# One-token attention over a 1 GB cache on one core: 64 KB rows, overlapping places, loops over heads

## The chip, the cores and the metric

The kernel runs on one core of a Trainium2 chip. The metric is the device time of one execution in microseconds. The kernel before has a median of 2582.4 us over three runs (2581.64 to 2582.49).

## The reference

One token attends to a cache of 65536 keys and values in each of 32 heads, a small gated MLP runs beside it, and a scalar gate mixes the two. Everything is bfloat16.

```python
B, Sq, D = 1, 1, 512
H, Sk, Dh = 32, 65536, 128          # k_cache, v_cache: [1, 32, 65536, 128], 537 MB each
F = 1792
q = (x @ wq) in 32 heads
p = softmax(q k^T * Dh ** -0.5)     # over 65536 keys, per head
a = (p v, heads side by side) @ wo
b = (silu(x @ w_gate) * (x @ w_up)) @ w_down
g = sigmoid((x * gate_w).sum(-1))
out = g * a + (1 - g) * b           # x = A_x everywhere; B_x is not used
```

K and V are 1073.7 MB, the five weights 13.9 MB. Each byte is read once, and each key and value is used for one query only.

## The kernel before

**Places and loads.** A ring of 20 slots of 8 KB per partition (160 KB) lies in SBUF. `plan_stream` (L25) writes the order of loads out by hand: wq first, then K in pieces of four slots (128 partitions with one contiguous row of 32 KB each, 4 MB), with w_gate, w_up and w_down behind the first K piece. V pieces of the same form follow two heads late, one after each K piece; wo comes just ahead of the last head's V, and the last V piece is cut into smaller ones. wo is read in rows of 1 KB (L184). SyncE walks this list (L206 to L228): before each load it waits until the ring's slots are free, which for K is when DVE has turned the piece (`ktdone`) and for V when PE has used it (`pvdone`).

**K.** Per unit of 64 keys a partition, DVE turns 32x32 blocks of 4-byte words, that is pairs of bf16 (L336, 4096 words a partition), into one of two `kt` buffers. PE then takes the turned K as the stationary operand, 128x128 at a time, and streams four columns of q past it (L412). `qd` holds q spread over columns so that the four partition groups of a turned block stay apart. A head's scores are 128x512 in PSUM, in one of two banks.

**Softmax.** Per head: DVE maximum over the scores (L310), GpSimd all-reduce over partitions (L245), ScalarE exponential with the row sum (L261), all-reduce of the sums (L247). DVE then shuffles the probabilities with 16 small copies (L320) into the layout in which V's rows stand.

**V.** V rows are the stationary operand, 128x128, and one column of probabilities streams past (L429); all 512 row groups of a head add up in one PSUM column. DVE scales the column by the inverse sum (L327).

**Projection, MLP, output.** The MLP runs early: up and gate after K unit 3, down after unit 4 (L375 to L390). The scaled head outputs are the stationary column in 32 matmuls of 512 columns against wo (L394), 31 of them between the last V pieces. One DVE instruction on one partition mixes both parts (L350) and ScalarE's queue stores 1x512 as one row (L264).

All engines run straight code: every head's instructions are written out. PE has 33062 matmuls and as many weight loads.

Of the kernel before, what the change touches and what calls it, by code (L numbers as in the profile page):

```python
# [5 lines left out]
P = 128  # L6
PC = 64
NR = PC // 4
UNIT = PC * 128
HU = UNIT // 2  # L10
RING = 20
ROW = 2
NSEM = 16

ALU = mybir.AluOpType
ACT = mybir.ActivationFunctionType
BF16 = mybir.dt.bfloat16
# [5 lines left out]


def plan_stream(H, NP):  # L25

    w = 2 * ROW  # L30
    per = 2 * NP // w
    ks = [("k", h, u * w, w) for h in range(H) for u in range(per)]
    vs = [("v", h, u * w, w) for h in range(H) for u in range(per)]
    vs = vs[:-1] + [("v", H - 1, 2 * NP - 4, 2), ("v", H - 1, 2 * NP - 2, 1), ("v", H - 1, 2 * NP - 1, 1)]
    lag = 2 * per
    items = [("wq", 0, 0, 4)]
    n = 0
    for i, it in enumerate(ks):
        items.append(it)
        if i == 0:  # L40
            items += [("wg", 0, 0, 2), ("wu", 0, 0, 2), ("wd", 0, 0, 2), ("pad", 0, 0, 2)]
        if i >= lag:
            items.append(vs[n])
            n += 1
    while n < len(vs):
        if vs[n][1:3] == (H - 1, 0):
            items.append(("wo", 0, 0, 4))
        items.append(vs[n])
        n += 1
    return items  # L50


def bass_gated_mix__mha_block_cached__swiglu_ffn__decode_kernel(
# [16 lines left out]
    Dc = D // P  # L70
    FC = F // P
    NP = S // P // PC
    SCALE = float(Dh) ** -0.5
    assert Dh == 128 and D == 512 and F % P == 0 and NP * PC == 512

    items = plan_stream(H, NP)

    dmas = []
    place = {}
    landed = {}  # L80
    owner = [None] * RING
    pos = 0
    for kind, h, u0, nu in items:
        done = 0
        while done < nu:
            k = min(nu - done, RING - pos % RING)
            slots = [(pos + j) % RING for j in range(k)]
            if kind != "pad":
                waits = [owner[s] for s in slots if owner[s] is not None]
                n = len(dmas)  # L90
                dmas.append((kind, h, u0 + done, k, slots[0], waits))
                for j in range(k):
                    place[(kind, h, u0 + done + j)] = slots[j]
                    landed[(kind, h, u0 + done + j)] = n
                    owner[slots[j]] = (kind, h, u0 + done + j)
            pos += k
            done += k
    kseq = {("k", h, u): h * NP + u // 2 for h in range(H) for u in range(2 * NP)}
    vseq = {("v", h, u): h * NP + u // 2 for h in range(H) for u in range(2 * NP)}

    with ExitStack() as ctx:
# [6 lines left out]
        def sem(name):  # L108
            return ctx.enter_context(nc.semaphore(name))

        psS = psum("psS", [P, 2, 512], F32)
        psO = psum("psO", [P, 2, 512], F32)
# [3 lines left out]
        psB = psum("psB", [P, 512], F32)  # L116

        ring = sb("ring", [P, RING * HU], BF16)
        kt = sb("kt", [P, 2, UNIT // 2], U32)
        sel = sb("sel", [P, 4, 128], BF16)  # L120
        ones1 = sb("ones1", [P, 2], BF16)
        xrow = sb("xrow", [P, D], BF16)
        gwrow = sb("gwrow", [P, D], BF16)
        xg = sb("xg", [P, D], F32)
        brow = sb("brow", [P, D], F32)
        fin = sb("fin", [P, D], BF16)
# [3 lines left out]
        qd = sb("qd", [P, H, 4, 4], BF16)  # L130
        hbuf = sb("hbuf", [P, 3, 16], F32)
        guT = sb("guT", [P, 16], BF16)
        mxs = sb("mxs", [P, H], F32)
        amx = sb("amx", [P, H], F32)
        nbias = sb("nbias", [P, H], F32)
        rsum = sb("rsum", [P, H], F32)
        Lt = sb("Lt", [P, H], F32)
        Li = sb("Li", [P, H], F32)
        oTn = sb("oTn", [P, H], BF16)
        pa = sb("pa", [P, 2, 512], BF16)  # L140
        pb = sb("pb", [P, 2, 512], BF16)

        s_x = sem("s_x")
        ds = [sem(f"ds{i}") for i in range(NSEM)]
        s_ones = sem("s_ones")
        s_sel0 = sem("s_sel0")
        s_sel = sem("s_sel")
        s_z = sem("s_z")
        s_e1 = sem("s_e1")
        s_xT = sem("s_xT")  # L150
        s_xTb = sem("s_xTb")
        s_q = sem("s_q")
        s_qTb = sem("s_qTb")
        s_qs = sem("s_qs")
        s_qd = sem("s_qd")
        s_h = sem("s_h")
        s_sig = sem("s_sig")
        s_gu = sem("s_gu")
        s_b = sem("s_b")
        s_dch = sem("s_dch")  # L160
        ktdone = sem("ktdone")
        qkdone = sem("qkdone")
        pvdone = sem("pvdone")
        s_mx = sem("s_mx")
        s_ar = sem("s_ar")
        s_nb = sem("s_nb")
        expdone = sem("expdone")
        s_pb = sem("s_pb")
        s_L = sem("s_L")
        s_otn = sem("s_otn")  # L170
        s_y = sem("s_y")
        s_fin = sem("s_fin")
        s_out = sem("s_out")

        xr_dram = A_x.rearrange("a b d -> (a b) d")
        out_dram = out.rearrange("a b d -> (a b) d")
        gw_dram = gate_w.rearrange("(a d) -> a d", a=1)
        w_dram = {
            "wq": A_wq.rearrange("(p c) n -> p (c n)", c=Dc),
            "wg": B_w_gate.rearrange("(p c) f -> p (c f)", c=Dc),  # L180
            "wu": B_w_up.rearrange("(p c) f -> p (c f)", c=Dc),
            "wd": B_w_down.rearrange("(p c) n -> p (c n)", c=FC),
        }
        wo_dram = A_wo.rearrange("(h d) n -> d h n", d=Dh)  # L184

        def at(key, n):
            s = place[key]
            return ring[:, s * HU:s * HU + n]

        wq_ap = at(("wq", 0, 0), Dc * H * Dh).rearrange("p (c n) -> p c n", c=Dc)  # L190
        wg_ap = at(("wg", 0, 0), Dc * F).rearrange("p (c m j) -> p c m j", c=Dc, j=FC)
        wu_ap = at(("wu", 0, 0), Dc * F).rearrange("p (c m j) -> p c m j", c=Dc, j=FC)
        wd_ap = at(("wd", 0, 0), FC * D).rearrange("p (c n) -> p c n", c=FC)
        wo_ap = at(("wo", 0, 0), H * D).rearrange("p (h n) -> p h n", h=H)
        ktb = [kt[:, b, :].bitcast(BF16).rearrange("p (j r m e) -> p j r m e", j=2, r=NR, e=2) for b in range(2)]

        def arrived(eng, key):
            n = landed[key]
            eng.wait_ge(ds[n % NSEM], 16 * (n // NSEM + 1))

        block = ctx.enter_context(nc.Block())

        @block.sync
        def _(sp):
            w = 2 * ROW
            for n, (kind, h, u0, k, s0, waits) in enumerate(dmas):  # L206
                need = {}
                for key in waits:
                    if key in kseq:
                        need["k"] = max(need.get("k", 0), kseq[key] + 1)  # L210
                    elif key in vseq:
                        need["v"] = max(need.get("v", 0), vseq[key] + 1)
                    else:
                        need[key[0]] = 1
                for key, s in (("wq", s_q), ("wg", s_h), ("wu", s_h), ("wd", s_b), ("k", ktdone), ("v", pvdone)):
                    if key in need:
                        sp.wait_ge(s, need[key])
                dst = ring[:, s0 * HU:(s0 + k) * HU]
                if kind in "kv":
                    cache = A_k_cache if kind == "k" else A_v_cache  # L220
                    src = cache[0, h].rearrange("(b p r) d -> b p (r d)", p=P, r=ROW * PC)[
                        u0 // w, :, (u0 % w) * HU:(u0 % w + k) * HU]
                elif kind == "wo":
                    dst, src = wo_ap, wo_dram
                else:
                    src = w_dram[kind]
                    dst = ring[:, s0 * HU:s0 * HU + src.shape[1]]
                sp.dma_start(dst, src).then_inc(ds[n % NSEM], 16)  # L228
                if n == 0:
                    sp.dma_start(xrow[0:1, :], xr_dram).then_inc(s_x, 16)  # L230
                    sp.dma_start(gwrow[0:1, :], gw_dram).then_inc(s_x, 16)

        @block.gpsimd
        def _(pool):
            nc.gpsimd.memset(sel[:], 0.0).then_inc(s_sel0, 1)
            pool.wait_ge(s_sel0, 1)
# [5 lines left out]
            last.then_inc(s_sel, 1)  # L242
            for h in range(H):
                pool.wait_ge(s_mx, h + 1)
                nc.gpsimd.partition_all_reduce(amx[:, h:h + 1], mxs[:, h:h + 1], P, RMAX).then_inc(s_ar, 1)  # L245
                pool.wait_ge(expdone, h + 1)
                nc.gpsimd.partition_all_reduce(Lt[:, h:h + 1], rsum[:, h:h + 1], P, RADD).then_inc(s_L, 1)  # L247
# [218 lines left out]
```

## Time and profile before

| | |
|---|---|
| runs, median | 2582.4 us |
| profiled execution, span from the first to the last instruction | 2580.2 us |
| DMA read from HBM | 1087.64 MB, 422 GB/s over the span |
| busy: PE, DVE, ACT, POOL | 952.7, 1308.7, 33.1, 25.9 us |
| mean granted TensorE clock | 0.516 |
| code fetched (queue 8) | 258 packets, 4.23 MB |
| K loads; V loads of 4 MB | 128; 127 |

The page cuts the span into 40 slices and gives busy tenths, the clock's tenths, the DMA engines' busy share and the rate in each. "DMA share" is a mean over 16 DMA engines. A load is landed when all of them have done their part. SPq rows are SyncE's issuing of loads, with the waits ahead of it. In a group's row "mean ns" is that of one instruction from its start to its modelled end; where instructions overlap, the spacing between their starts is shorter.

### The profile page before, as it was taken

The numbers are of one execution on the slowest core, as the hardware profiler recorded it, in microseconds if no ns is written. First come the engines' busy times: TensorE is split into PE (matmuls) and PEld (weight loads), VectorE is DVE, ScalarE is ACT, GpSimd is POOL, SyncE is SP. The second block draws the span as 40 slices with busy tenths as digits, with TensorE's granted clock in tenths as the row PEclk, the third lists the DMA queues.
The fourth block names the chain that finished last, engine by engine and source line by source line (L and its number), as shares of the span: only waits on it lengthen the run. The fifth ranks groups of instructions, "written<-read, shape, count | busy, mean of one in ns | idle before, by whom it ended". The sixth has DMA issues, their size and how long they took to land.

```text
span 2580.2 us, 67894 instructions
## 1 busy us (share of the span) xinstructions
PE 952.7 (37%) x33062; PEld 915.5 (35%) x33062; DVE 1308.7 (51%) x883; ACT 33.1 (1%) x99; POOL 25.9 (1%) x73
## 2 busy tenths in 40 slices
PE   2443333333333333333334333433343333333334
PEld 2343333333333333333334333333343333333333
DVE  3955554455454545544554445445445554455430
ACT  0000000000000000000000000000000000000000
POOL 0000000000000000000000000000000000000000
PEclk9555555555555555555555555555555555555555
DMA  9999999999999999999999999999999999999997
GB/s 412 423 431 428 429 429 430 429 430 431 428 428 428 430 429 430 430 429 429 428 429 427 427 426 426 425 424 426 429 425 424 425 424 425 427 423 425 424 392 314
DMA packets 42117, 1091.99 MB, mean 423 GB/s; under 512 B 4211, under 2 KB 8310, under 8 KB 8310
## 3 DMA queue, kind: packets, MB, share of 16 engines
q1 hardware_dynamic: 41844, 1087.65, 98.7%
q8 instruction: 258, 4.23, 0.7%
q14 instruction: 13, 0.11, 0.0%
q10 hardware_dynamic: 2, 0.00, 0.0%
HBM read 1087.64 MB, written 0.00 MB: 422 GB/s over the span
## 4 chain that ended last, share of the span: by engine, by line
DMA 74%; issue 9%; PE 8%; DVE 8%; SPq 0%; DVEq 0%
DMA ring<-in_A_k_cache_dram 61%; DMA ring<-in_A_v_cache_dram 14%; DVE kt L336 7%; PE psO L429 5%; PE psS L412 2%; PE psY L394 0%; PE psM L380 0%; PE psB L388 0%; DVE mxs L310 0%; DVE pb L320 0%; SPq L228 0%; DVE Li L325 0%; DVE brow L306 0%; DVE fin L350 0%; DVE oTn L327 0%
## 5 line engine op out<-in xcount | busy, mean ns | idle before, releaser
L336 DVE STREAM_TRANSPOSE kt<-ring 128x4096 uint32<-128x4096 uint32 x256 | 1128.4, 4430 | 1147.8 <-DMA ring<-in_A_k_cache_dram 1147.7
L412 PE MATMUL psS<-qd,kt 128*128 128x4 bf16 x16384 | 478.0, 166 | 1408.1 <-DVE kt L336 1408.1
L412 PEld LDWEIGHTS psS<-qd,kt 128*128 128x128 bf16 x16384 | 456.8, 104 | 1429.5 <-DVE kt L336 1429.5
L429 PE MATMUL psO<-pb,ring 128*128 128x1 bf16 x16384 | 463.8, 165 | 201.7 <-issue 143.1
L429 PEld LDWEIGHTS psO<-pb,ring 128*128 128x128 bf16 x16384 | 451.8, 104 | 207.6 <-issue 164.6
L320 DVE COPY pb<-pa 32x128 bf16<-32x128 bf16 x512 | 154.3, 301 | 10.2 <-PE psO L429 3.7
L327 DVE TENSOR_SCALAR oTn<-psO,Li 128x1 bf16<-128x1 f32 x32 | 7.1, 221 | 83.0 <-PE psO L429 81.9
L257 ACT ACTIVATE nbias<-amx 128x1 f32<-128x1 f32 x32 | 6.5, 203 | 2390.3 <-POOL amx L245 2390.3
L245 POOL PARTITION_ALL_REDUCE amx<-mxs x32 | 11.3, 353 | 2412.6 <-DVE mxs L310 2412.6
L261 ACT ACTIVATE pa<-psS,nbias 128x512 bf16<-128x512 f32 x32 | 22.0, 688 | 1.0
L310 DVE TENSOR_REDUCE mxs<-psS 128x1 f32<-128x512 f32 x32 | 20.9, 653 | 2.0 <-PE psS L412 2.0
L247 POOL PARTITION_ALL_REDUCE Lt<-rsum x32 | 12.3, 386 | 36.4 <-ACT pa L261 36.4
L394 PE MATMUL psY<-ring,oTn 128*1 128x512 bf16 x32 | 10.3, 492 | 0.4 <-DVE oTn L327 0.4
L281 DVE CUSTOM_DVE_ANT_0 xg<-xrow,gwrow 1x512 f32<-1x512 bf16 x1 | 0.9, 874 | 12.7 <-DMA gwrow<-in_gate_w_dram 12.7
L380 PE MATMUL psM<-xTb,ring 128*128 128x1 bf16 x112 | 6.9, 198 | 0.0
L380 PEld LDWEIGHTS psM<-xTb,ring 128*128 128x128 bf16 x112 | 6.8, 159 | 0.0
L261 ACT ACTIVATION_READ_ACCUMULATOR pa<-psS,nbias 128x1 f32 x32 | 6.2, 193 | 0.0
L394 PEld LDWEIGHTS psY<-ring,oTn 128*1 128x1 bf16 x32 | 3.1, 101 | 6.6 <-issue 4.2
L359 PE MATMUL psM<-ones,xrow 1*128 1x1 bf16 x4 | 0.3, 171 | 14.0 <-DMA gwrow<-in_gate_w_dram 14.0
L359 PEld LDWEIGHTS psM<-ones,xrow 1*128 1x128 bf16 x4 | 0.2, 113 | 14.0 <-DMA gwrow<-in_gate_w_dram 14.0
L388 PE MATMUL psB<-ring,guT 128*1 128x512 bf16 x14 | 4.8, 515 | 0.0
L325 DVE RECIPROCAL Li<-Lt 128x1 f32<-128x1 f32 x32 | 4.0, 124 | 0.0
(29 smaller groups left out, 18.2 us busy)
## 6 DMA issues: line engine op xcount, KB each, us to landing
ring<-in_A_k_cache_dram SPq DMA_DIRECT2D x128, 4096.0 KB, 43.5
ring<-in_A_v_cache_dram SPq DMA_DIRECT2D x127, 4096.0 KB, 41.0
ring<-in_A_wq_dram SPq DMA_DIRECT2D x1, 4096.0 KB, 12.8
ring<-in_A_wo_dram SPq DMA_DIRECT2D x1, 4096.0 KB, 46.1
ring<-in_A_v_cache_dram SPq DMA_DIRECT2D x1, 2048.0 KB, 38.5
ring<-in_A_v_cache_dram SPq DMA_DIRECT2D x2, 1024.0 KB, 43.1
ring<-in_B_w_gate_dram SPq DMA_DIRECT2D x1, 1792.0 KB, 26.1
ring<-in_B_w_up_dram SPq DMA_DIRECT2D x1, 1792.0 KB, 29.8
```

What stands on the lines that cost most here:

```text
L245: nc.gpsimd.partition_all_reduce(amx[:, h:h + 1], mxs[:, h:h + 1], P, RMAX).then_inc(s_ar, 1)
L247: nc.gpsimd.partition_all_reduce(Lt[:, h:h + 1], rsum[:, h:h + 1], P, RADD).then_inc(s_L, 1)
L257: nc.scalar.mul(nbias[:, h:h + 1], amx[:, h:h + 1], -SCALE).then_inc(s_nb, 1)
L261: nc.scalar.activation(pa[:, h % 2, :], psS[:, h % 2, :], ACT.Exp, bias=nbias[:, h:h + 1], scale=SCALE, accum_out=rsum[:, h:h + 1]).then_i ...
L310: nc.vector.reduce_max(mxs[:, h:h + 1], psS[:, h % 2, :], AX_X).then_inc(s_mx, 1)
L320: last = nc.vector.tensor_copy(dst, sr)
L327: nc.vector.tensor_scalar(oTn[:, h:h + 1], psO[:, h % 2, h:h + 1], Li[:, h:h + 1], None, ALU.mult).then_inc(s_otn, 1)
L336: nc.vector.transpose(o, src).then_inc(ktdone, 1)
L380: last = nc.tensor.matmul(psM[:, o + j:o + j + 1], w[:, c, :, j], xTb[:, c:c + 1], start=(c == 0), stop=(c == Dc - 1))
L394: last = nc.tensor.matmul(psY[0:1, :], oTn[:, h:h + 1], wo_ap[:, h, :], start=(h == 0), stop=(h == H - 1))
L412: last = nc.tensor.matmul(psS[:, h % 2, col:col + 4], ktb[i % 2][:, je // 2, r, :, je % 2], qd[:, h, je, :], start=(je == 0), stop=(je == 3))
L429: last = nc.tensor.matmul(psO[:, h % 2, h:h + 1], vt[:, r * Dh:(r + 1) * Dh], pb[:, h % 2, col:col + 1], start=(col == 0), stop=(col == 511))
```

## The change

- **Rows and places.** K and V are read as two halves a head, each 128 partitions with one contiguous row of 64 KB (8 MB). There are two K places, at bytes 0 to 64 K and 32 to 96 K of a partition, and two V places, at 96 to 160 K and 112 to 176 K. The places of a pair overlap, so a half may be loaded once the other half's part in the shared bytes has been used. DVE takes each first half's upper part first (`A_ORDER`), and PE's values are cut at 64 and 192 rows, with a semaphore increment at each cut, so that the shared bytes come free first. The first head's K comes as two pieces of 32 KB rows and one of 64 KB.
- **Order of loads.** wq, head 0's K, then K, V, K, V with V one head late; then wo, one row group of wo for the last head, w_gate, the last head's first V half, and w_up, the last V pieces and w_down.
- **Loops.** On PE and DVE heads 1 to 31 are a loop of 31 rounds. The other engines stay written out.
- **K streams.** Now K's turned words are the moving operand, 512 wide, and q is the stationary one: a window of `zq` that puts the four scores of a chunk into its own four rows of PSUM. A chunk is 16 keys a partition, with one DVE transpose of 1024 words and four matmuls; there are four `kt` buffers. A head has 128 score matmuls where it had 512. Scores, probabilities and `psO` have one buffer each.
- **Shuffle.** One DVE transpose of 128x512 replaces the 16 copies.
- **wo in 32 KB rows.** Head outputs are kept as four partial blocks in `lt`, turned on PE by an identity at the end, and projected with 128 matmuls of one column each, whose result lies over partitions as 128x4. The last head's is added apart.
- **MLP last.** Up and gate run between the last V pieces, down is the last work of PE. Its result adds into the same PSUM columns, since the gate is folded into the scale of the heads' outputs and into the MLP's hidden vector.
- **Output.** ScalarE copies 128x4 and stores it as 128 rows of 8 bytes.

```diff
-PC = 64
-UNIT = PC * 128
-RING = 20
-ROW = 2
+CH = 16
+NB = 4
+K_A, K_B = 0, 32 * KB
+V_A, V_B = 96 * KB, 112 * KB
+RING = 176 * KB
+V_CUT_A = 64
+V_CUT_B = 192
...
+    A_ORDER = list(range(NCH // 2, NCH)) + list(range(NCH // 2))
+    B_ORDER = list(range(NCH))
...
+        kv_dram = {"k": A_k_cache[0].rearrange("h (u p r) d -> h u p (r d)", u=2, p=P),
+                   "v": A_v_cache[0].rearrange("h (u p r) d -> h u p (r d)", u=2, p=P)}
...
+            for r in range(1, H):
+                sp.wait_ge(sm["ktd"], PER * r + NCH // 2)
+                place("k", r, 1, "s_kb")
+                sp.wait_ge(sm["pvd"], 4 * (r - 1) + 1)
+                place("v", r - 1, 1, "s_vb")
+                if r < L:
+                    sp.wait_ge(sm["ktd"], PER * r + NCH + NCH // 2)
+                    place("k", r + 1, 0, "s_ka")
+                    sp.wait_ge(sm["pvd"], 4 * (r - 1) + 3)
+                    place("v", r, 0, "s_va")
+            sp.wait_ge(sm["ktd"], PER * L + NCH)
+            load(at(WO, 32 * D), A_wo.rearrange("(p j) n -> p (j n)", j=32), "s_wo")
+            sp.wait_ge(sm["ktd"], PER * H)
+            load(at(WO1, D), A_wo[L * Dh:H * Dh, :], "s_wo1")
+            load(at(WG, Dc * F), B_w_gate.rearrange("(p c) f -> p (c f)", c=Dc), "s_wg")
+            sp.wait_ge(sm["pvd"], 4 * (L - 1) + 3)
+            place("v", L, 0, "s_va")
+            last = kv_dram["v"][L, 1]
+            sp.wait_ge(sm["s_wod"], 1)
+            load(at(P3, 128 * Dh), last[:, 0:128 * Dh], "s_p3")
+            load(at(WU, Dc * F), B_w_up.rearrange("(p c) f -> p (c f)", c=Dc), "s_wu")
+            load(at(P1, 64 * Dh), last[:, 128 * Dh:192 * Dh], "s_p1")
+            sp.wait_ge(sm["pvd"], 4 * L)
+            load(at(P2, 64 * Dh), last[:, 192 * Dh:256 * Dh], "s_p2")
+            load(at(WD, FC * D), B_w_down.rearrange("(p c) n -> p (c n)", c=FC), "s_wd")
...
+            nc.scalar.copy(fin[:], psY[:, 0:Dc]).then_inc(sm["s_fin"], 1)
+            act.dma_start(out_dram, fin[:]).then_inc(sm["s_out"], 16)
...
+            with nc.Fori(1, H, engines=[ET.DVE], head_slot={ET.DVE: 0}) as i:
+                take_q(i)
+                dve.wait_ge(sm["s_ka"], i * 16)
+                for n, c in enumerate(A_ORDER):
+                    turn(K_A, c, n, i * PER + (n - NB + 1))
+                    if n == 0:
+                        dve.wait_ge(sm["s_otn"], i)
+                        dve.wait_ge(sm["s_L"], i)
+                        nc.vector.reciprocal(Li, Lt).then_inc(sm["s_li"], 1)
+                dve.wait_ge(sm["s_kb"], i * 16)
+                for n, c in enumerate(B_ORDER):
+                    turn(K_B, c, NCH + n, i * PER + (NCH + n - NB + 1))
+                head_max(i * PER + PER)
+                dve.wait_ge(sm["pvd"], i * 4)
+                dve.wait_ge(sm["s_li"], i)
+                nc.vector.tensor_scalar(lt[:, bass.ds(i * 4 - 4, 4, P + 1)], psO[:, 0:1].to_broadcast([P, 4]),
+                                        Li, sc[:, 3:4], ALU.mult, ALU.mult).then_inc(sm["s_otn"], 1)
+                head_turn(i + 1)
...
+            def scores(n, c, need, first, stop):
+                pe.wait_ge(sm["ktd"], need)
+                for je in range(4):
+                    last = nc.tensor.matmul(psS[:], zw[je][c], ktb[n % NB][:, je // 2, :, je % 2],
+                                            start=first and je == 0, stop=stop and je == 3)
+                last.then_inc(sm["qkd"], 1)
...
+            with nc.Fori(1, H, engines=[ET.PE], head_slot={ET.PE: 0}) as i:
+                pe.wait_ge(sm["s_zq"], i + 1)
+                pe.wait_ge(sm["s_exp"], i)
+                for n, c in enumerate(A_ORDER):
+                    scores(n, c, i * PER + (n + 1), n == 0, False)
+                pe.wait_ge(sm["s_pb"], i + 1)
+                pe.wait_ge(sm["s_otn"], i)
+                pe.wait_ge(sm["s_va"], i * 16)
+                values(V_A, 0, range(V_CUT_A, ROWS), True, False)
+                values(V_A, 0, range(0, V_CUT_A), False, False)
+                for n, c in enumerate(B_ORDER):
+                    scores(NCH + n, NCH + c, i * PER + (NCH + n + 1), False, n == NCH - 1)
+                pe.wait_ge(sm["s_vb"], i * 16)
+                values(V_B, 1, range(0, V_CUT_B), False, False)
+                values(V_B, 1, range(V_CUT_B, ROWS), False, True)
```

More of the change, by code (lines that the diff above doesn't have):

```diff
@@ L22 @@
 RADD = bass.bass_isa.ReduceOp.add
[L25 to L50, printed above, removed]
 def bass_gated_mix__mha_block_cached__swiglu_ffn__decode_kernel(
@@ L71, in bass_gated_mix__mha_block_cached__swiglu_ffn__decode_kernel @@
     FC = F // P
-    NP = S // P // PC
+    ROWS = S // (2 * P)
+    NCH = ROWS // CH
     SCALE = float(Dh) ** -0.5
[L74 to L99, printed above, removed]
+    assert Dh == 128 and D == 512 and F % P == 0 and ROWS == 256 and H == 32
+    L = H - 1
+    A_ORDER = list(range(NCH // 2, NCH)) + list(range(NCH // 2))
+    B_ORDER = list(range(NCH))
+    FIRST = [(0, c) for c in B_ORDER] + [(1, c) for c in A_ORDER]
+    PER = 2 * NCH
     with ExitStack() as ctx:
@@ L160, in bass_gated_mix__mha_block_cached__swiglu_ffn__decode_kernel @@
[L160 to L173, printed above, removed]
+        st = sb("st", [P, 8], F32)
+        mxs, amx, nbias, rsum, Lt, Li = (st[:, i:i + 1] for i in range(6))
@@ L204, in _ @@
         def _(sp):
[L205 to L231, printed above, removed]
@@ L263, in _ @@
-            act.wait_ge(s_fin, 1)
-            act.dma_start(out_dram, fin[0:1, :]).then_inc(s_out, 16)
-            act.wait_ge(s_out, 16)
-        kunits = [(h, u) for h in range(H) for u in range(NP)]
+                act.wait_ge(sm["s_ar"], h + 1)
+                nc.scalar.mul(nbias, amx, -SCALE).then_inc(sm["s_nb"], 1)
+                act.wait_ge(sm["s_nb"], h + 1)
+                if h:
+                    act.wait_ge(sm["s_pb"], h + 1)
+                nc.scalar.activation(pa[:], psS[:], ACT.Exp, bias=nbias, scale=SCALE,
+                                     accum_out=rsum).then_inc(sm["s_exp"], 1)
@@ L345, in _ @@
-            head_max(H - 1)
-            head_shuffle(H - 1)
-            for h in range(H - 3, H):
-                head_norm(h)
-            dve.wait_ge(s_y, 1)
-            nc.vector.scalar_tensor_tensor(out=fin[0:1, :], in0=psY[0:1, :], scalar=sc[0:1, 3:4],
-                                           in1=brow[0:1, :], op0=ALU.mult, op1=ALU.add).then_inc(s_fin, 1)
+                                           accum_out=sc[0:1, 0:1]).then_inc(sm["s_z"], 1)
+            dve.wait_ge(sm["s_xT"], 1)
@@ new lines, in head_max, with head_turn @@
+            def head_max(done):
+                dve.wait_ge(sm["qkd"], done)
+                nc.vector.reduce_max(mxs, psS[:], AX_X).then_inc(sm["s_mx"], 1)
+            def head_turn(exps):
+                dve.wait_ge(sm["s_exp"], exps)
+                nc.vector.transpose(pb[:], pa[:]).then_inc(sm["s_pb"], 1)
+            take_q(0)
+            for n, (u, c) in enumerate(FIRST):
+                if u == 0 and c == 0:
+                    dve.wait_ge(sm["s_k0a"], 16)
+                if u == 0 and c == NCH // 2:
+                    dve.wait_ge(sm["s_k0b"], 16)
+                if n == NCH:
+                    dve.wait_ge(sm["s_k0c"], 16)
+                turn(64 * KB * u, c, n, n - NB + 1 if n >= NB else None)
@@ L437, in _, with values @@
-            project(H - 1)
+            last.then_inc(sm["s_qs"], 1)
+            def scores(n, c, need, first, stop):
[4 more added lines that the diff above has]
+                last.then_inc(sm["qkd"], 1)
+            def values(base, u, rows, first, stop):
+                for i, r in enumerate(rows):
+                    col = (r % CH) * 32 + NCH * u + r // CH
+                    last = nc.tensor.matmul(psO[:, 0:1], at(base + r * 256, Dh), pb[:, col:col + 1],
+                                            start=first and i == 0, stop=stop and i == len(rows) - 1)
+                last.then_inc(sm["pvd"], 1)
@@ new lines, in _ @@
+            last.then_inc(sm["s_wod"], 1)
+            pe.wait_ge(sm["s_pb"], H + 1)
+            pe.wait_ge(sm["s_va"], 16 * H)
+            values(V_A, 0, range(ROWS), True, False)
+            pe.wait_ge(sm["s_p3"], 16)
+            values(P3, 1, range(0, 128), False, False)
+            pe.wait_ge(sm["s_wg"], 16)
+            pe.wait_ge(sm["s_wu"], 16)
+            for j in range(FC):
+                for w, o in ((wg_ap, 64), (wu_ap, 80)):
+                    for c in range(Dc):
+                        last = nc.tensor.matmul(psM[:, o + j:o + j + 1], w[:, c, :, j], xTb[:, c:c + 1],
+                                                start=(c == 0), stop=(c == Dc - 1))
@@ new lines, in _ @@
+            last.then_inc(sm["s_h"], 1)
+            pe.wait_ge(sm["s_p1"], 16)
+            values(P1 - 128 * 256, 1, range(128, 192), False, False)
+            pe.wait_ge(sm["s_p2"], 16)
+            values(P2 - 192 * 256, 1, range(192, 256), False, True)
+            pe.wait_ge(sm["s_wo1"], 16)
+            pe.wait_ge(sm["s_o31"], 1)
+            for b in range(Dc):
+                nc.tensor.matmul(psY[:, b:b + 1], wo1_ap[:, :, b], o31[:, 0:1], start=False, stop=False,
+                                 skip_group_check=True)
@@ L441 @@
+            pe.wait_ge(sm["s_gu"], 1)
+            pe.wait_ge(sm["s_wd"], 16)
+            for j in range(FC):
+                for b in range(Dc):
+                    last = nc.tensor.matmul(psY[:, b:b + 1], wd_ap[:, j, :, b], guT[:, j:j + 1], start=False,
+                                            stop=(j == FC - 1 and b == Dc - 1), skip_group_check=True)
+            last.then_inc(sm["s_y"], 1)
 _INS = ['A_x', 'A_k_cache', 'A_v_cache', 'A_wq', 'A_wo', 'B_x', 'B_w_gate', 'B_w_up', 'B_w_down', 'gate_w']
```

344 lines of the change are left out of this document (140 added, 204 removed).

## The prediction

> **What bounds the kernel now.** I read the page first: engines, slices, DMA queues, chain.
>
> ```profile
> PE 952.7 (37%) x33062; PEld 915.5 (35%) x33062; DVE 1308.7 (51%) x883; ACT 33.1 (1%) x99; POOL 25.9 (1%) x73
> ...
> PEclk9555555555555555555555555555555555555555
> DMA  9999999999999999999999999999999999999997
> GB/s 412 423 431 428 429 429 430 429 430 431 428 428 428 430 429 430 430 429 429 428 429 427 427 426 426 425 424 426 429 425 424 425 424 425 427 423 425 424 392 314
> ...
> q1 hardware_dynamic: 41844, 1087.65, 98.7%
> q8 instruction: 258, 4.23, 0.7%
> ...
> DMA 74%; issue 9%; PE 8%; DVE 8%; SPq 0%; DVEq 0%
> ```
>
> The transfers set the time: they are busy in every slice, and no engine is over 51%. The rate is about 430 GB/s in the first half and 425 in the second, and 258 packets of code travel beside the data. So the next question is what rate the same transfers reach when nothing disturbs them. The DMA view cut to windows answers it: first the slices of 3 to 100 us, then the totals of 1400 to 2400 us, then the slices of 2400 to 2580 us.
>
> ```profile
> GB/s 432 432 392 432 433 432 432 329 426 420 432 437 426 457 426 432 432 432 432 432 432 432 432 439 419 250 324 419 432 432 432 426 419 432 432 426 419 432 432 439
> ...
> DMA packets 14654, 425.43 MB, mean 425 GB/s; under 512 B 1617, under 2 KB 1617, under 8 KB 1617
> q1 hardware_dynamic: 14548, 423.73, 99.3%
> q8 instruction: 101, 1.65, 0.7%
> ...
> DMA  9999998999999999999999995444599999999920
> GB/s 448 408 419 459 437 404 379 433 444 401 455 397 430 451 404 426 451 430 397 459 426 372 374 372 222 211 201 176 196 409 430 437 437 411 437 415 404 390 91 0
> ```
>
> Undisturbed slices show 432 GB/s, in 32 KB rows. The 1000 us in the middle of the run move 423.73 MB of data, 423.7 GB/s: 1.95% less, (432/423.7 - 1). The last row tells who loses it. For five slices of 4.5 us, some 22 us, busy share and rate fall to half (222, 211, 201, 176, 196): half of the 16 DMA engines have finished all that was queued and the other half is still behind. A load counts as landed only when all engines have done their share, so the slower half sets the time. My reading is that it carries the code packets. SyncE's own rows show why the quick half can't run further ahead: it issues only when a place of the ring is free, and at the end six loads take it 33.53 us.
>
> ```profile
> SPq L228 <- DVE kt L336: 1584.7, 127, 15.2
> SPq L228 <- PE psO L429: 800.9, 121, 38.3
> ...
> 2498.85 33.53 SPq L228 DMA_DIRECT2D ring<-in_A_v_cache_dram  x6
> ```
>
> The span in these terms: 1087.65 MB at 432 GB/s is 2517.7 us. What is left of 2580.2 is 62.5 us: a tail of 6.4 (below), 2.8 for wo in 1 KB rows (below), 2.0 before the first bytes, and about 51 of lag. The first windows row gives the 2.0: 20 us at 388 GB/s are 7.76 MB, which take 18.0 at 432.
>
> ```profile
> 0.00:20.00 20.00, 4.15 (x136) 3.88 (x136) 2.68 (x11) 1.49 (x2) 2.26 (x9) 1.00 0.94 388
> ```
>
> As a check on the lag, 1.95% of 2517.7 is 49.1. I use 49: 0.19 us for each of the 258 packets.
>
> **The change, part by part.**
>
> *PE and DVE loop over heads.* PE's 2 x 33062 instructions over 258 packets are 256 instructions a packet: the straight code is fetched once. After the change PE has, outside its loop, 1081 matmuls with their weight loads, 2162 instructions or 9 packets; the loop body has 128 score and 512 value matmuls, 1280 instructions, 5 packets, and with its waits touches 6. If the body stays loaded, some 15 packets are left, and the lag goes from 49 to 3 us: **-46**. No row shows a loop; the other end, all fetched anew, is a rival below.
>
> *64 KB rows.* K and V have 32768 rows of 32 KB now and 16384 of 64 KB then: 1024 fewer per DMA engine. What a row costs beside its bytes, I take from the narrowest rows there are, wo's:
>
> ```profile
> DMA packets 996, 2.69 MB, mean 336 GB/s; under 512 B 15, under 2 KB 943, under 8 KB 943
> q1 hardware_dynamic: 996, 2.69, 87.6%
> ```
>
> From 2502 to 2510 us 1 KB rows run at 336 GB/s: 48.8 ns a row on each of 16 engines against 37.9 at 432, so 11 ns more; corrected for the busy share of 87.6% (384 GB/s) 5 ns. So the gain is 5 to 11 us, and 0 if a row is cut in two on the way. I take 8 ns: **-8**. The Trainium skill, DMA: Bandwidth & Descriptors, section Where 436 GB/s comes from, puts a ceiling of 435.2 GB/s on the 16 ports together; by that the gain could not pass 18 us, and the 432 here stands just below it.
>
> *wo in 32 KB rows.* 4.19 MB at 336 are 12.5 us, at 432 9.7: **-2.8**. A second copy of the last head's rows (0.13 MB) costs **+0.3**.
>
> *Overlapping places.* Five places of 4 MB become four of 8 MB that overlap in pairs, and a load is 19.4 us (8.39 MB at 432). The order is K, V, K, V, so a head takes 77.7 us. Does the queue run dry? I need what PE and DVE take.
>
> ```profile
> L336 DVE STREAM_TRANSPOSE kt<-ring 128x4096 uint32<-128x4096 uint32 x256 | 1128.4, 4430 | 1147.8 <-DMA ring<-in_A_k_cache_dram 1147.7
> L412 PE MATMUL psS<-qd,kt 128*128 128x4 bf16 x16384 | 478.0, 166 | 1408.1 <-DVE kt L336 1408.1
> ...
> L320 DVE COPY pb<-pa 32x128 bf16<-32x128 bf16 x512 | 154.3, 301 | 10.2 <-PE psO L429 3.7
> ...
> L310 DVE TENSOR_REDUCE mxs<-psS 128x1 f32<-128x512 f32 x32 | 20.9, 653 | 2.0 <-PE psS L412 2.0
> ...
> L388 PE MATMUL psB<-ring,guT 128*1 128x512 bf16 x14 | 4.8, 515 | 0.0
> ...
> 2524.31 3.57 PE L429 MATMUL psO<-pb,ring 128*128 128x1 bf16 x128 [6.14 <-DMA ring<-in_A_v_cache_dram]
> 2559.15 0.13 PEld L394 LDWEIGHTS psY<-ring,oTn 128*1 128x1 bf16 x1 [0.30 <-issue]
> 2559.57 0.13 PEld L394 LDWEIGHTS psY<-ring,oTn 128*1 128x1 bf16 x1 [0.30 <-issue]
> ...
> 2564.24 3.32 PEld L394 LDWEIGHTS psY<-ring,oTn 128*1 128x1 bf16 x16 [0.27 <-issue]
> ```
>
> DVE's transposes go from 4096 to 1024 words: a quarter of 4430 is 1.11 us, and I take 1.25 with a fixed part. PE streams K's words 512 wide: the projections of before show 0.43 us from one to the next at half clock and 3.32/16 = 0.21 after some 6 us of dense work. Four make a chunk: 1.71 or 0.84 us. A V row takes 3.57/128 = 28 ns.
>
> Let a first K half land at 0, at half clock, the worse end. Its upper 8 chunks are turned by about 13 us, and the next K half is issued; V keeps the queue until 19.4. All 16 are scored by 28.5; V's first 192 rows take 5.4, so the next V is issued at 34, and K keeps the queue until 38.8. The other K half then lands; its scores end at 67.5 and 192 V rows at 73, and the queue has work until 77.7. The least spare time is 4.7 us; at full clock DVE leads (20 us a half) and it is 9 to 10. A load's issue is one instruction on SP, and about half as many are issued as now. So I cost the places at **0**; the cover is the load before. If it goes, every microsecond late comes twice per head, 62 us in all.
>
> *Per-head work.* One 128x512 transpose replaces the 16 copies of L320 (16 x 301 ns = 4.8 us); the nearest row, L310 with as many elements, has 0.65. Maximum, all-reduces and exponential end before V is done. DVE's head turn waits for V's values, until about 75 us at half clock; queued behind it are the next head's transposes, whose K lands at 77.7. **0**, hidden under that load.
>
> *MLP last.* Its three loads (5.5 MB, 12.7 us) keep their bytes; they move on SP's queue behind the last K and between the pieces of the last V. The up and gate matmuls lie under the pieces P1 and P2 (2.1 MB, 4.9 us each). Only w_down's 56 are bare. Tail of before, and a row of such column reads:
>
> ```profile
> 57.27 2.90 PE L380 MATMUL psM<-xTb,ring 128*128 128x1 bf16 x46
> ...
> 2573.80 3.12 PE L429 MATMUL psO<-pb,ring 128*128 128x1 bf16 x104 [1.78 <-issue]
> 2577.03 0.22 DVE L327 TENSOR_SCALAR oTn<-psO,Li 128x1 bf16<-128x1 f32 x1 [48.75 <-PE psO L429]
> ...
> 2577.93 0.74 DVE L350 SCALAR_TENSOR_TENSOR fin<-psY,sc,brow 1x512 bf16<-1x512 f32 x1 [0.68 <-PE psY L394]
> 2578.70 0.50 ACTq L264 DMA_DIRECT2D out_dram<-fin  x1
> ```
>
> Before, 6.4 us pass from 2573.8 to the end. Then: 56 at 2.90/46 = 63 ns make 3.5, one copy of 128x4 about 0.3, output 1.5 as now: 5.5 with the steps between. The 128 rows of 8 bytes on 16 engines may give half a microsecond back. **-0.6**.
>
> The sum against the profiled 2580.2: -46 - 8 - 2.8 + 0.3 + 0 + 0 - 0.6 = 2523.1. The runs' median 2582.4 is 2.2 above the profiled span, so **2525** for the runs.
>
> **The rivals.**
>
> *The loop's code is fetched anew in every round.* 31 rounds of 6 packets and 9 outside make 195, and 195 x 0.19 = 37 us of lag where I left 3: 2559. For it: the trace shows code fetched strictly ahead and once, and nothing that shows it kept. Against it: the body is 6 packets long, so little needs to be kept. The jump back is hidden: PE has some 3 us spare at the end of a round at half clock and 12 at full clock. The Trainium skill, Runtime: NRT & Kernel Launch, section Instruction fetch mechanics, speaks for this rival: it calls the instruction memory a FIFO with no cache to profit from and says a taken branch out of its window forces a fetch. By that rule the time would be 2559; no run here shows it yet. Chance 0.25.
>
> *The lag isn't the code's.* Then half the engines stay slow, and only rows and tail gain, 0 to 12 us: 2571 to 2582. Against it: undisturbed slices reach 432 on all engines, with dips between. Chance 0.07.
>
> *PE becomes the bound.* K's words are read at a stride of two elements, which no 512-wide row of the trace does. A head holds 128 of these matmuls and 14.3 us of values: at 0.43 us 69.3 of 77.7. From 0.49 us on PE sets the period; at 0.515 (the mean of one in L388, if that were the spacing) a head takes 66 + 14.3 + about 3 of waits = 83: 5.3 x 31 = 164 us, 2688, slower than before. Against it: 0.43 is the spacing already at half clock, and denser work doubles the clock. Chance 0.08.
>
> **How the numbers follow.** My forecast has the remaining 0.60; its own range is 2513 to 2538 (rows at 0 or 11, one or two packets fetched per round). The range 2513 to 2565 takes in the refetched loop and leaves out the other two rivals and the edges, about 0.2. A difference under 0.2%, 5 us, can't be told from none. Slower: PE's rival and a little for unseen mishaps, 0.09. Same: the part of the unexplained lag in which rows gain nothing, 0.03. Faster: the rest, 0.88.
>
> **What would show it.** Code packets: about 15 with my forecast, 195 with the first rival. Data rate: 432 to 435 GB/s in all slices, with no half-share stretch near the end; about 427 with the first rival. DVE should wait for K in every head, and PE's score matmuls should stand 0.43 us or less apart. Data packets near 17,000 mean 64 KB rows go whole; near 34,000, that they are cut. It would be wrong if the queue ran dry between places: slices under 400 GB/s, with SP's waits ending late.

## The result and the profile after

The changed kernel takes 2526.78 us (median of four runs, 2526.64 to 2526.92) where the kernel before, on the same chip, takes 2582.44. The ratio is 0.9784, with a 95% interval of 0.9771 to 0.9798. The prediction said 2525. The profiled execution spans 2524.8 us against 2580.2.

First the page of the changed kernel: engines, slices, queues, chain.

```profile
PE 1566.0 (62%) x20826; PEld 833.2 (33%) x20922; DVE 1222.3 (48%) x1207; ACT 33.2 (1%) x100; POOL 26.3 (1%) x75
...
PEclk9777677677676776777767767767677677677675
DMA  9999999999999999999999999999999999999998
GB/s 421 423 432 431 432 432 435 435 432 432 435 436 435 432 432 432 434 435 433 432 433 435 434 433 433 432 432 437 435 432 432 434 435 434 432 433 432 437 429 362
...
q1 hardware_dynamic: 19732, 1087.78, 99.7%
q8 instruction: 14, 0.23, 0.0%
...
DMA 74%; DVE 16%; issue 7%; PE 2%; DVEq 0%; another core or an unknown queue 0%; SPq 0%; ACT 0%; POOL 0%
```

The transfers still set the time, at the same 74% of the chain, but they are faster: 431 to 437 GB/s from the third slice to the 38th, where the first half of the kernel before had about 430 and its second half about 425. Code packets fell from 258 to 14. A code packet holds 16 KB (4.23 MB in 258 packets before); below, such a piece of code is called a block. Data packets fell from 41844 to 19732, so 64 KB rows travel whole: 16128 of the packets are such rows, and most of the others are the loads' own 4-byte counts. PE is busier than before (1566 us against 953) and this costs nothing.

Next the DMA view of the changed kernel: totals of 1400 to 2400 us, then the slices of 2400 us to the end (3.1 us each).

```profile
DMA packets 7446, 433.46 MB, mean 433 GB/s; under 512 B 832, under 2 KB 832, under 8 KB 832
q1 hardware_dynamic: 7446, 433.46, 100.2%
...
DMA  8999999899998989889899998997989899999100
GB/s 377 503 419 398 461 398 461 377 503 440 398 482 377 461 357 503 388 367 472 368 418 566 398 467 357 524 419 325 472 377 457 376 425 435 419 416 382 46 6 0
```

In this millisecond not one code packet moves, and the data run at 433.5 GB/s; before it was 423.7. The stretch at half share that stood near the end before (222 211 201 176 196) is gone: all DMA engines now end together. The 503, 566 and the like beside lower values come from slices of 3.1 us, in which only some 20 rows of 64 KB begin.

### The profile page after: what moved, and what is told of

Read it like the earlier page. It is cut to its first block, busy times and chain, and to the rows that moved or that the text cites. A ratio compares the mean times of both kernels' runs of the same rounds, so it can differ in the third digit from the quotient of the medians.

```text
span 2524.8 us, 45802 instructions
## 1 busy us (share of the span) xinstructions
PE 1566.0 (62%) x20826; PEld 833.2 (33%) x20922; DVE 1222.3 (48%) x1207; ACT 33.2 (1%) x100; POOL 26.3 (1%) x75
## 3 DMA queue, kind: packets, MB, share of 16 engines
q1 hardware_dynamic: 19732, 1087.78, 99.7%
## 4 chain that ended last, share of the span: by engine, by line
DMA 74%; DVE 16%; issue 7%; PE 2%; DVEq 0%; another core or an unknown queue 0%; SPq 0%; ACT 0%; POOL 0%
DMA ring<-in_A_k_cache_dram 71%; DVE kt L253 15%; DMA ring<-in_A_v_cache_dram 2%; DMA ring<-in_A_wo_dram 2%; PE psS L337 1%; DVEq L250 0%; PE psO L344 0%; PE psY L378 0%; DVE st L283 0%; SPq L128 0%; PE psY L408 0%; ACT pa L202 0%; DVE st L257 0%; POOL st L186 0%
## 5 line engine op out<-in xcount | busy, mean ns | idle before, releaser
L337 PE MATMUL psS<-kt,zq 128*128 128x512 bf16 x4000 | 1116.8, 425 | 902.3 <-DVE kt L253 880.1
L253 DVE STREAM_TRANSPOSE kt<-ring 128x1024 uint32<-128x1024 uint32 x1024 | 1163.1, 1206 | 983.0 <-DMA ring<-in_A_k_cache_dram 983.0
L337 PEld LDWEIGHTS psS<-kt,zq 128*128 128x128 bf16 x4096 | 387.9, 105 | 1604.7 <-DVE kt L253 1132.8
L344 PE MATMUL psO<-pb,ring 128*128 128x1 bf16 x16384 | 433.3, 164 | 34.3 <-DMA ring<-in_A_v_cache_dram 20.1
L344 PEld LDWEIGHTS psO<-pb,ring 128*128 128x128 bf16 x16384 | 427.7, 99 | 64.1 <-issue 34.1
L290 DVE TENSOR_SCALAR lt<-psO,st,sc 128x4 f32 x31 | 9.1, 294 | 197.4 <-PE psO L344 197.4
L257 DVE TENSOR_REDUCE st<-psS 128x1 f32<-128x512 f32 x32 | 22.1, 692 | 37.4 <-PE psS L337 37.4
L186 POOL PARTITION_ALL_REDUCE st<-st x32 | 11.3, 353 | 2382.6 <-DVE st L257 2382.6
L261 DVE STREAM_TRANSPOSE pb<-pa 128x512 bf16<-128x512 bf16 x32 | 22.4, 701 | 1.6 <-ACT pa L202 1.6
L202 ACT ACTIVATE pa<-psS,st 128x512 bf16<-128x512 f32 x32 | 22.0, 687 | 1.0
L190 POOL PARTITION_ALL_REDUCE st<-st x32 | 12.3, 385 | 36.4 <-ACT pa L202 36.4
## 6 DMA issues: line engine op xcount, KB each, us to landing
ring<-in_B_w_down_dram SPq DMA_DIRECT2D x1, 1792.0 KB, 47.1
```

Source lines behind the costliest of these rows:

```text
L186: nc.gpsimd.partition_all_reduce(amx, mxs, P, RMAX).then_inc(sm["s_ar"], 1)
L190: nc.gpsimd.partition_all_reduce(Lt, rsum, P, RADD).then_inc(sm["s_L"], 1)
L202: nc.scalar.activation(pa[:], psS[:], ACT.Exp, bias=nbias, scale=SCALE, accum_out=rsum).then_inc(sm["s_exp"], 1)
L253: nc.vector.transpose(o, src).then_inc(sm["ktd"], 1)
L257: nc.vector.reduce_max(mxs, psS[:], AX_X).then_inc(sm["s_mx"], 1)
L261: nc.vector.transpose(pb[:], pa[:]).then_inc(sm["s_pb"], 1)
```

## The experiments

Times are medians of runs; those of the kernel before on the same chips were 2581.94 to 2582.73.

**PE's rounds written out.**

```diff
-            with nc.Fori(1, H, engines=[ET.PE], head_slot={ET.PE: 0}) as i:
+            for i in range(1, H):
```

> The changed kernel with PE's 31 rounds written out; all else as changed. Code theory: PE's 41,700 instructions are 163 packets instead of 14, at 0.19 us of lag each: +28 us on 2526.8, about 2555; the rate in the middle falls from 433 to about 428 GB/s. Rival (half of the DMA engines were slow for another reason, which the new places or rows removed): 2527, whatever the number of code packets.

Measured: 2554.73 us, ratio to before 0.9895 (0.9878 to 0.9911). Page and DMA view (1400 to 2400 us) of this kernel:

```profile
q8 instruction: 163, 2.67, 0.4%
...
DMA packets 7411, 429.12 MB, mean 429 GB/s; under 512 B 816, under 2 KB 816, under 8 KB 816
q1 hardware_dynamic: 7348, 428.08, 99.7%
```

149 more code packets cost 27.95 us, 0.188 each, and the data rate falls to 428. Rows, places and order are those of the change, so the rival that these removed the lag falls. PE itself stops for code here, 31 times in this millisecond, 4.7 us at the longest and 98 us in all, so straight code does not always lie ready ahead of it. But the DMA engines are busy all the while (99.7% data and 0.4% code), so the loss is theirs and not PE's.

**The kernel before with less code.** Only one of the four score matmuls of each group is left.

```diff
-                            for je in range(4):
+                            for je in (0,):
...
-                                                        qd[:, h, je, :], start=(je == 0), stop=(je == 3))
+                                                        qd[:, h, je, :], start=True, stop=True)
```

> The kernel before with one of the four score matmuls of each group left (the scores are then a quarter of the sum, and the output is another): 41,548 PE instructions instead of 66,124, about 162 code packets instead of 258. Code theory: the lag falls from 49 to 31 us: 2582.4 - 18 = 2564. Rival (lag not from code; PE is off the path): 2582.

Measured: 2562.89 us, 0.9925 (0.9909 to 0.9942). Page and the same window:

```profile
q8 instruction: 162, 2.65, 0.4%
...
DMA packets 14793, 429.83 MB, mean 430 GB/s; under 512 B 1640, under 2 KB 1640, under 8 KB 1640
q1 hardware_dynamic: 14724, 428.74, 99.9%
```

96 packets fewer gain 19.05 us, 0.198 each, in the old places and with old rows. From the other side it is the same price. PE does less work here too. SyncE does wait for PE to free places of V (265.5 us of 1400 to 2400 us in the kernel before), but always with loads still queued: the DMA engines were busy all that time (99.3% data and 0.7% code, in the prediction's view). The first experiment changes the code alone.

**Rows of 32 KB in the new places.**

```diff
-                load(at(byte, ROWS * Dh), kv_dram[kind][h, u], s)
+                for z in range(2):
+                    load(at(byte + 32 * KB * z, half), kv_dram[kind][h, u][:, half * z:half * (z + 1)], s)
...
-                dve.wait_ge(sm["s_ka"], i * 16)
+                dve.wait_ge(sm["s_ka"], i * 32)
```

The waits on the other three places count 32 in the same way.

> The changed kernel, each 64 KB place loaded by two loads of 32 KB rows. Row theory: 1024 more rows per DMA engine at 5 to 11 ns: +5 to +11 us, I say 2535. Rival (rows of 32 KB and more cost nothing beside their bytes): 2527. The two loads share one place and one wait, so nothing else should move.

Measured: 2535.52 us, 0.9819 (0.9803 to 0.9835). Page and window:

```profile
q1 hardware_dynamic: 37732, 1087.79, 99.8%
...
DMA packets 14823, 431.70 MB, mean 432 GB/s; under 512 B 1648, under 2 KB 1648, under 8 KB 1648
```

18000 more packets, the loads' own 4-byte counts among them, are 1125 for each of 16 DMA engines and cost 8.74 us: 7.8 ns a packet. The kernel before, run beside each of the two, differs by 0.5 us between them. The rate returns to the 432 GB/s that the undisturbed slices of the kernel before showed.

**wo alone, in the kernel before.**

```diff
-        wo_dram = A_wo.rearrange("(h d) n -> d h n", d=Dh)
+        wo_dram = A_wo.rearrange("(d h) n -> d h n", d=Dh)
```

> The kernel before with wo read in 32 KB rows (each head is then multiplied with other rows of wo, so the output is another): the row term of the prediction, -2.8 us, about 2579.6. Rival (the wo load lies where the quick half of the DMA engines waits anyway, so only the slow half's share counts): the slow half moves the same rows, so the two differ only if the rate of narrow rows was misread; 2582 then.

Measured: 2580.6 us, 0.9995 (0.9985 to 1.0004). That is 1.3 us less, and the interval reaches from -3.9 to +1.0: it holds the forecast and zero. This term stays open.

**Places without the overlap's early release.** SyncE waits for the whole half.

```diff
-                sp.wait_ge(sm["ktd"], PER * r + NCH // 2)
+                sp.wait_ge(sm["ktd"], PER * r + NCH)
...
-                sp.wait_ge(sm["pvd"], 4 * (r - 1) + 1)
+                sp.wait_ge(sm["pvd"], 4 * (r - 1) + 2)
...
-                    sp.wait_ge(sm["ktd"], PER * r + NCH + NCH // 2)
+                    sp.wait_ge(sm["ktd"], PER * r + 2 * NCH)
...
-                    sp.wait_ge(sm["pvd"], 4 * (r - 1) + 3)
+                    sp.wait_ge(sm["pvd"], 4 * (r - 1) + 4)
```

> The changed kernel, but SyncE waits for all of a half before it loads the place that overlaps it (K after 16 chunks instead of 8, V after 256 rows instead of 192); places and loads are the same. Cover theory (the load before hides the release): a K half is turned 18.2 us after it lands, and the trace has 2.0 us from issue to first byte, together 20.2; the V load ahead lasts 19.35 for the late DMA engines and ends 1.9 sooner for the early ones. So each of 62 K loads comes 1 to 3 us late: +60 to +170 us, I say 2627. V stays hidden. Rival (enough is queued anyway, the cut into overlapping parts buys nothing): 2527.

Measured: 2630.23 us, 1.0196 (1.0180 to 1.0212): about 2% slower than the kernel before. First the changed kernel's timeline around one head, then that of this experiment and its DMA window.

```profile
1700.46 1.25 DVE L253 STREAM_TRANSPOSE kt<-ring 128x1024 uint32<-128x1024 uint32 x1 [11.49 <-DMA ring<-in_A_k_cache_dram]
...
1707.67 7.32 PEld L337 LDWEIGHTS psS<-kt,zq 128*128 128x128 bf16 x33 [0.23 <-issue]
1709.68 0.33 SPq L128 DMA_DIRECT2D ring<-in_A_k_cache_dram  x1
...
1724.71 0.33 SPq L128 DMA_DIRECT2D ring<-in_A_v_cache_dram  x1
1739.15 18.14 DVE L253 STREAM_TRANSPOSE kt<-ring 128x1024 uint32<-128x1024 uint32 x16 [20.49 <-DMA ring<-in_A_k_cache_dram]
...
1748.31 0.33 SPq L128 DMA_DIRECT2D ring<-in_A_k_cache_dram  x1
...
1777.87 1.25 DVE L253 STREAM_TRANSPOSE kt<-ring 128x1024 uint32<-128x1024 uint32 x1 [11.56 <-DMA ring<-in_A_k_cache_dram]
```

```profile
1693.50 1.25 DVE L253 STREAM_TRANSPOSE kt<-ring 128x1024 uint32<-128x1024 uint32 x1 [12.97 <-DMA ring<-in_A_k_cache_dram]
...
1711.74 0.33 SPq L128 DMA_DIRECT2D ring<-in_A_k_cache_dram  x1
...
1733.71 18.14 DVE L253 STREAM_TRANSPOSE kt<-ring 128x1024 uint32<-128x1024 uint32 x16 [22.01 <-DMA ring<-in_A_k_cache_dram]
...
DMA packets 7167, 417.21 MB, mean 417 GB/s; under 512 B 800, under 2 KB 800, under 8 KB 800
```

With the early release the next K half is issued 9.2 us after the last one lands (1709.68 against 1700.46), while V has some 10 us of queue left. Without it the issue comes after 18.2 us, and the halves stand 40.2 us apart instead of 38.7. The loss of 103 us is 1.7 for each of 62 loads. So the overlap is worth more than everything else in the change, and in the sum it rightly stood at zero: it keeps a loss away that four large places would otherwise bring.

**How much code a loop may have.** Three versions lengthen PE's round with 320, 190 or 100 matmuls into a scratch column that nothing uses (the first diff; only the number differs); one puts two heads into a round.

```diff
                 values(V_B, 1, range(V_CUT_B, ROWS), False, True)
+                for _ in range(320):
+                    nc.tensor.matmul(psQ[:, 0, 0:1], sel[:, 0, :], qTb[:, 0:1], start=True, stop=True)
```

```diff
-            with nc.Fori(1, H, engines=[ET.PE], head_slot={ET.PE: 0}) as i:
+            with nc.Fori(1, H - 1, 2, engines=[ET.PE], head_slot={ET.PE: 0}) as i:
+                one_head(i)
+                one_head(i + 1)
+            one_head(H - 1)
```

> The changed kernel with two heads in a round of PE's loop (15 rounds and one head written out): the body is some 2580 instructions, over 10 packets. Theory that only so much code stays loaded (the tensor engine's 2048 instructions in the Trainium skill's account): every round is fetched anew, about 165 packets and +28 us, 2555, with a stall of a few us at each jump back that the wait for K hides. Rival (any loop stays loaded, or a round's code isn't dropped while a part of it fits): far fewer packets, 2527 to 2540.

> The changed kernel with 320 further matmuls on PE at the end of each round, which write a scratch column and are used by nothing: a body of some 1930 instructions, 7.5 packets instead of 5. They take 320 x 28 ns = 9 us of the 11.6 us that PE waits there. If a body up to 2048 instructions stays loaded: 14 to 20 packets and 2527. If the code ahead of the jump pushes the body's start out: 100 to 250 packets, 2545 to 2570.

> As the run with 320 further matmuls per round, with 190 of them: a body of some 1670 instructions, 6.5 packets, so 7 touched; 5.3 us of the 11.6 that PE has spare. The 7.5 packets were not kept. If 7 are kept: about 15 code packets and 2527. If not: some 8 a round, 250 in all, 45 us of lag and stalls of 2 to 4 us at each packet's end, 2570 to 2700.

> The same with 100 further matmuls: some 1490 instructions, 5.8 packets, so 6 touched, as many as the changed kernel's body touches. If what counts is the packets touched: about 15 code packets, 2527. If the changed kernel's body is kept only because it is hardly over 5: fetched anew, 220 packets, 2565 or more.

Code packets by the pages, one line each: 100 matmuls more, 190 more, 320 more, two heads.

```profile
q8 instruction: 15, 0.25, 0.0%
```

```profile
q8 instruction: 16, 0.26, 0.0%
```

```profile
q8 instruction: 286, 4.69, 0.6%
```

```profile
q8 instruction: 192, 3.15, 0.5%
```

| instructions in a round | code packets | us |
|---|---|---|
| 1290 (the change) | 14 | 2526.78 |
| 1490 (100 more) | 15 | 2526.8 (one run) |
| 1670 (190 more) | 16 | 2527.2 (one run) |
| 1930 (320 more) | 286 | 2817.63, ratio 1.0909 (1.0892 to 1.0926) |
| 2580 (two heads) | 192 | 2566.85, ratio 0.9939 (0.9924 to 0.9954) |

A body of 6.5 packets stays loaded, one of 7.5 is fetched anew in every round, some 9 packets each. So the limit lies between 1670 and 1930 instructions for a body that begins at a block's start, below the 2048 from which two of the expectations set out. The versions with 100 and 190 more matmuls also give PE 3100 and 5890 matmuls more in the whole run, at 15 and 16 packets, and cost nothing that one run shows: it is the fetched code that costs, not the instructions. What I expected of 7.5 packets, at most 2570, was far too little. The rows that show why are, of the version with 1930, the waits of PE in 1400 to 2400 us, and from its timeline the turning of the second K half in two successive rounds, with the end of PE's round and its jump back between them.

```profile
PE psO L344 <- issue: 103.5, 34, 4.2
PE psS L337 <- issue: 85.2, 11, 7.9
PE psQ L368 <- issue: 81.1, 22, 4.0
...
1506.17 18.14 DVE L253 STREAM_TRANSPOSE kt<-ring 128x1024 uint32<-128x1024 uint32 x16 [14.71 <-DMA ring<-in_A_k_cache_dram]
...
1544.63 3.57 PE L368 MATMUL psQ<-qTb,sel 128*128 128x1 bf16 x128 [3.74 <-issue]
...
1551.94 2.35 PE L368 MATMUL psQ<-qTb,sel 128*128 128x1 bf16 x82 [3.73 <-issue]
...
1562.03 17.23 PE L337 MATMUL psS<-kt,zq 128*128 128x512 bf16 x63 [7.75 <-issue]
...
1592.69 18.14 DVE L253 STREAM_TRANSPOSE kt<-ring 128x1024 uint32<-128x1024 uint32 x16 [14.56 <-DMA ring<-in_A_k_cache_dram]
```

PE stops 2 to 4 us at the end of most packets among its values and fillers, and 7.8 at the jump back, with nothing else to wait for. That these are the ends of packets shows in the spacing: 128 matmuls, with their weight loads 256 instructions, lie between two stops. A round takes 86.5 us instead of 77.4, and 31 rounds make 282 of the 291 us: PE, waiting for its own code, is the bound, and the lag of the DMA engines no longer shows: their queue runs dry (data keep them busy 90.4% of 1400 to 2400 us). Two heads in a round have the same stops (2 to 4.6 us) but no filler, so that PE has time for most of them; there the lag (178 packets at 0.19 are 34 us) leaves 6 of the 40 us unexplained by it.

**A version that beats both.** DVE's loop is not moved to a block's start, and the result is turned into one row before the store.

```diff
-            with nc.Fori(1, H, engines=[ET.DVE], head_slot={ET.DVE: 0}) as i:
+            with nc.Fori(1, H, engines=[ET.DVE]) as i:
...
+            pe.wait_ge(sm["s_fin"], 1)
+            for b in range(Dc):
+                last = nc.tensor.matmul(psQ[0:1, b, :], fin[:, b:b + 1], ident[:], start=True, stop=True)
...
+            nc.scalar.copy(frow[0:1, :].rearrange("p (m b) -> p m b", b=Dc),
+                           psQ[0:1, :, :].rearrange("p b m -> p m b")).then_inc(sm["s_fin"], 1)
...
-            act.dma_start(out_dram, fin[:]).then_inc(sm["s_out"], 16)
+            act.dma_start(out_row, frow[0:1, :]).then_inc(sm["s_out"], 16)
```

> The changed kernel with DVE's loop not moved to the start of a fetch block, and the result turned into one row of 512 by four PE matmuls with the identity and stored as one row. Theory: the 5.7 us that DVE stands still as it enters its loop make the second K half 2.4 us late, once: -2.4; the store of 128 rows of 8 bytes takes 3.9 us where one row took 1.5, and the turning costs some 1.3: -1.1. Together 2523. Rival (the loop is entered no sooner, or its body falls across more blocks and is fetched in each round): 2526 to 2545.

Measured: 2523.49 us (2523.01 to 2524.07), 0.9772 (0.9759 to 0.9786). Its runs and those of the changed kernel don't overlap: 3.3 us less. The changed kernel's timeline where DVE enters its loop, then this version's:

```profile
74.58 0.71 DVE L261 STREAM_TRANSPOSE pb<-pa 128x512 bf16<-128x512 bf16 x1 [1.60 <-ACT pa L202]
...
80.98 0.20 DVE L246 COPY zq<-qd 128x16 bf16 x1 [5.69 <-issue]
...
90.34 0.33 SPq L128 DMA_DIRECT2D ring<-in_A_k_cache_dram  x1
```

```profile
75.01 0.16 DVE L250 COPY zq<-qd 128x16 bf16 x1
...
84.26 0.33 SPq L129 DMA_DIRECT2D ring<-in_A_k_cache_dram  x1
```

The stop of 5.69 us is gone and the K load is issued 6.1 us sooner, before the V load ahead of it has ended: the changed kernel's DMA view of 3 to 100 us has one slice at 189 GB/s there, 2.4 us long, and this version's has none under 378. The end of both follows in the same order: changed kernel with its DMA view, then this version.

```profile
2471.12 0.43 SPq L128 DMA_DIRECT2D ring<-in_B_w_down_dram  x1
...
2518.32 2.00 PE L408 MATMUL psY<-guT,ring 128*128 128x1 bf16 x56
2520.36 0.16 ACT L207 CAST fin<-psY 128x4 bf16<-128x4 f32 x1 [8.39 <-PE psY L408]
2520.55 0.37 ACTq L209 DMA_DIRECT2D out_dram<-fin  x1
...
ring<-in_B_w_down_dram SPq DMA_DIRECT2D x1, 1792.0 KB, 47.1
...
out_dram<-fin ACTq DMA_DIRECT2D x1, 1.0 KB, 3.9
```

```profile
2516.11 2.00 PE L412 MATMUL psY<-guT,ring 128*128 128x1 bf16 x56 [0.66 <-DMA ring<-in_B_w_down_dram]
...
2518.36 0.58 PE L417 MATMUL psQ<-ident,fin 128*1 128x128 bf16 x4 [0.25 <-ACT fin L208]
2518.97 0.57 ACT L210 CAST frow<-psQ 1x512 bf16<-1x512 f32 x1 [0.67 <-PE psQ L417]
2519.58 0.50 ACTq L213 DMA_DIRECT2D out_dram<-frow  x1
```

128 rows of 8 bytes take 3.9 us to land and the span ends at 2524.8, 4.25 us after their issue. One row ends 1.5 us after its issue (2521.1 - 2519.6). The turning costs 1.2 us (from 2518.30, the cast's end, to 2519.54), so the store's part of the gain is some 1.5. The rest is the loop's entry: w_down's matmuls begin 2.2 us sooner (2516.11 against 2518.32). Together these are the 3.7 us between the two profiled spans; 2.4 and 1.1 were expected.

## Why the prediction was right

- **The bound and the lag.** Right, and in size: -46 was forecast from 0.19 us a packet. The experiments give 0.188 (27.95 us for 149) and 0.198 (19.05 for 96), and 14 packets are left where I said 15; 244 packets fewer at these prices are 46 to 48 us. So the lag comes and goes with the number of packets, from both sides.
- **Which engines carry the code.** That the packets travel on the very DMA engines that lag, which the prediction called its reading, can be read from the trace, which keeps the start and the duration of every packet though no view lists them. In the half-share stretch of the kernel before, 8 data packets are in flight at a time, and while a code packet is in flight there are 7. The count falls by one in the same way for all seven code packets in such stretches: three in the kernel before and two each in the versions with wo alone and with less code. The size fits as well. From 200 to 2400 us a code packet takes 1.06 us, and at the end of each of the 222 a data packet begins that takes 0.5 us longer than the usual 1.21; 1.56 us spread over 8 engines are 0.195 a packet. Open is what most of the other long data packets do: 305 stand beside 101 code packets from 1400 to 2400 us, and none in the changed kernel.
- **The two rates of the kernel before.** Code comes at the same pace early and late (80 packets in 200 to 1000 us, 101 in 1400 to 2400), yet data run at 427.6 GB/s first (342.10 MB in 800 us) and at 423.7 later. The first is close to the mean of 432 and 423.7, as if the quick half still ran undisturbed; the second would be the slow half's rate, and the half-share stretch what the quick half had gained by then. Such a stretch need not appear: with PE's rounds written out, 163 packets cost 28 us, and yet only 8 packets are in flight for no more than some 3 us near the end. My reading is that two places of a kind let the quick half run less far ahead.
- **64 KB rows.** Forecast -8, measured 8.74, from a bracket of 5 to 11 ns a row that narrow rows gave. The bracket was sound; that a value from its middle came so close is luck.
- **wo.** Forecast -2.8; the run alone says -1.3 with an interval that holds both zero and the forecast. Open.
- **Overlapping places at zero.** Right in the middle of the run. The half clock was the worse end; PE's clock is 0.72 in the mean, the transposes lead with 18.1 us a half, and the release leaves some 10 us. The sentence on a lost cover held too: 103 us for 62 loads. Wrong at one spot: the step that counts a load's issue did not look at the entry into DVE's loop. It stops DVE for 5.69 us, once, and the first second-half K comes late.
- **The tail.** Forecast -0.6, measured +0.2: from the last load's landing (2471.1 + 47.1 = 2518.2) to the end are 6.6 us, against 6.4 before. Two terms were mis-sized and in part cancel, which is luck. w_down's 56 matmuls take 2.0 us instead of 3.5: the row they were priced by is of the up and gate matmuls, which still take 61 ns each here (112 in 6.86 us), while w_down's take 36. And the store of 8-byte rows, put at half a microsecond more without a row for it, ends 4.25 us after its issue where one row took 1.5, so it costs 2.75 more.
- **The sum.** 2523.1 was forecast for the profiled span and 2524.8 came: the tail's 0.8 and the loop's entry (2.2) are more than the difference, the rows' 0.7 goes the other way, and wo is not known to this precision. The forecast's own range, 2513 to 2538, comes out of the terms named for it only in part: rows at 11 ns give 2522 and not 2513, and rows at 0 with one packet fetched a round 2539, with two 2545. The measured time lies inside either way.
- **The rival of code fetched anew** did not come about, since this body stays loaded. Its price, 2559, was too low for a body that doesn't: I wrote that the jump back is hidden, and left out that PE stops at every packet's end. The Trainium skill, Runtime: NRT & Kernel Launch, section Instruction fetch mechanics, says that nothing is gained from a cache and that a taken branch out of the window, which it puts at two pages, forces a fetch. The runs here differ from the first part: 31 rounds of a body of up to 6.5 packets moved 14 to 16 packets in all. They differ from the second as well for these bodies, whose jump goes back over five packets or more, and agree with it for bodies of 7.5 and 10 packets.
- **The rival of PE as the bound.** Not here. PE's score matmuls stand 0.43 us apart at half clock and 0.22 at full (33 weight loads in 7.32 us), so the stride of two in K's words does not show. It did come about where PE waited for its own code.

## What to carry to other kernels

When a kernel is bound by loads, look at whether all DMA engines end together: a stretch at half share near the end and a rate that drops after the early slack is used up say that something else travels on some of them, though a missing stretch does not show that nothing does. Straight code on a busy engine can be that something, here 0.19 us per 16 KB of it; a loop that stays loaded removes it, and a body a little too long costs more than straight code. Larger places need their release planned against the transfer ahead, and a loop's entry, like a store of tiny rows, belongs into the sum.

## What was not expected of the hardware

- Code packets travelled on the 8 of 16 DMA engines that lagged, as far as the seven show that can be told apart. A packet took 1.06 us, and the data packet behind it 0.5 us longer than others.
- PE keeps a loop of 1670 instructions loaded and one of 1930 not; the latter made the kernel 9% slower than before, through stops of 2 to 4 us at the ends of packets and 7.8 us at each jump back.
- Entering a loop whose head had been moved to a fetch block's start stopped DVE for 5.69 us beside full DMA queues.
- A store of 1 KB as 128 rows of 8 bytes needs 3.9 us to land; as one row it is done in about 1.5.
- A data packet costs 7.8 ns beside its bytes even at 32 to 64 KB, and 433.5 GB/s was reached with 64 KB rows.
